# Channel 128's copy and rest on GpSimd instead of VectorE, and the weight decode's last two pieces in chunk 11 instead of chunks 9 and 10

## The chip, the cores and the metric

The kernel runs on one core of one Trainium2 chip. The metric is device time in microseconds (us) of one execution. TensorE is called PE below, VectorE DVE, ScalarE ACT, GpSimd POOL; SP is the engine from which all DMAs here are issued.

## What is computed

The input has two batches of 3136 positions by 256 channels. Three blocks follow one another (cut to what matters):

```python
def reference(**kw):
    # 1: Fourier mixing along the sequence
    X = np.fft.rfft(x, axis=1)
    Yr = Xr @ w_r - Xi @ w_i + b_r;  Yi = Xr @ w_i + Xi @ w_r + b_i
    Y = soft_threshold(Yr, 0.01) + 1j * soft_threshold(Yi, 0.01)
    x = np.fft.irfft(Y, n=3136, axis=1)
    # 2: normalise, two matrix products with a ReLU between, add
    xn = (x - mean) / np.sqrt(var + 1e-6) * g_ln
    x = x + np.maximum(xn @ w_ch1, 0.0) @ w_ch2
    # 3: x plus the real part of a 2D FFT of x, then the same again with other weights
    u = x + np.real(np.fft.fft(np.fft.fft(x, axis=1), axis=2))
    un = (u - mean) / np.sqrt(var + 1e-6)
    return u + np.maximum(un @ w_ch1, 0.0) @ w_ch2
```

## The kernel before

The sequence length is 49 x 64, and each Fourier transform is two matrix products with tables. The program is recorded in one order, and a list scheduler then sets the order on each engine, so moving a step also shifts its neighbours a little.

**The two MLPs.** `mlp1` (block 2) has 13 chunks, numbered 0 to 12, of four tiles of 128 rows each, but for chunk 6 (three tiles) and chunk 7 (two). `mlp2` (block 3) has 13 more. `run_mlp` (L869) goes over them. In each chunk `l1(f)` (L619) makes one of eight slices f of the hidden layer: six matmuls into a PSUM buffer psa, of which there are three. Then ACT writes the rounded ReLU h (L631), and DVE writes the rest that the rounding left (L632), which gives psa back to PE. `l2(i)` (L639) sums the eight slices into psb, and DVE adds the result to the input (L649). The next chunk is normalised by `prep` (L570: a chain of small DVE operations L576 to L585 with one ACT step between) and transposed by `trans` (L599).

**The decode.** The weights of `mlp2` come as 64-bit numbers in eight pieces. `decode64` (L500) turns a piece into two float parts with eight DVE operations of 128x512 (L506 to L514), into the tile r2b. `MLP2_AT` (L26) says in which chunk of `mlp1`, and after which slice f of `l1`, each piece is decoded. The two pieces that the change moves fill the part of r2b that holds `w_ch2`, which is first read by `l2` of `mlp2` chunk 0.

**Stage 4.** `Stage98` (L334) makes the first transform of block 3, for batch 0 from the end of chunk 7 on, in which SP issues its first loads, and for batch 1 during `mlp2` from its chunk 0 on. Its 16 steps each load 98x512 values (L348), fold channels c and 256 - c with three POOL operations (`split`, L360 to L362), round on ACT (L364), take the rest on POOL (L365, seen in the trace as L210), multiply on PE into a buffer psc, of which there are three (`mm3r`, L220 to L222), copy out on ACT (L404) and store. Channel 128 has no partner. `middle` (L369) loads it alone for all steps (98x32 values, tile m), and `middle2` (L376), run with step 0, copies and splits it, multiplies it (L381), and copies the product to the tile `mid`; POOL puts two columns of `mid` into every step's output (L405).

An engine works through its own queue in order. What stands behind a waiting instruction on that engine waits too.

Of the kernel before, what the change touches and what calls it, by code (L numbers as in the profile page):

```python
# [22 lines left out]
STAGE3_AT = (0,) * 16 + (3, 3, 3, 3, 3, 1)  # L23
CONST_AT = (0, 0, 1, 2, 2, 3, 4, 5, 6, 8)
MLP1_AT = (5, 8, 10, 12, 13, 14, 15, 18)
MLP2_AT = ((4, 6), (5, 2), (5, 6), (6, 2), (6, 6), (7, 3), (9, 3), (10, 6))  # L26
STAGE3_END = 3
STAGE3_MLP = ((0, 0), (0, 1), (0, 2), (0, 3), (1, 0), (1, 1), (1, 2), (1, 3),
              (2, 0), (2, 1), (2, 2), (2, 3), (3, 0))
# [25 lines left out]
NQ = 98  # L55
# [107 lines left out]
def fourier_moe_kernel(ctx, tc, x, w_r, w_i, b_r, b_i, g_ln, w11, w12, w21, w22,  # L163
                       t_ca, t_cam, t_cim, t_cb, t_ci, t_cb0, t_ci0, t_cd, t_ident, out):
    nc = tc.nc
# [9 lines left out]
    def psum(tag):  # L175
        return pp.tile([128, 512], F32, tag="ps" + tag, name="ps" + tag, bufs=ps_bufs[tag])
# [24 lines left out]
    def a_copy(o, i, scale=1.0):  # L201
        nc.scalar.activation(out=o, in_=i, func=AF.Copy, scale=scale)

    def v_copy(o, i):
        nc.vector.tensor_copy(o, i)
# [3 lines left out]
    def sub(eng, o, a, b):  # L209
        ins = eng.tensor_tensor(out=o, in0=a, in1=b, op=ALU.subtract)  # L210
        mark["pool" if eng is nc.gpsimd else "dve"] = getattr(ins, "ins", ins)

    def mm3(ps, lh, ll, rh, rl, first, last):
        nc.tensor.matmul(out=ps, lhsT=lh, rhs=rh, start=first, stop=False)  # L214
        nc.tensor.matmul(out=ps, lhsT=lh, rhs=rl, start=False, stop=False)  # L215
        nc.tensor.matmul(out=ps, lhsT=ll, rhs=rh, start=False, stop=last)  # L216
# [117 lines left out]
    class Stage98:  # L334
# [40 lines left out]

        def middle2(self):  # L376
            t, hl = self.mid_in
            v_copy(hl[:, 0], t)
            sub(nc.vector, hl[:, 1], t, hl[:, 0])
            ps = psum(self.tag)  # L380
            mm3(ps[0:NQ, 0:32], cs_h, cs_l, hl[:, 0], hl[:, 1], True, True)  # L381
            self.mid = wk.tile([NQ, 32], F32, tag="mid", name="mid", bufs=1)
            v_copy(self.mid, ps[0:NQ, 0:32])

        def start(self):
            self.middle()
# [531 lines left out]
    def after(k, i, f):  # L918

        def g():  # L920
            with tc.issue_after(mlp1[k].rest[i]):
                f()
        return g
# [8 lines left out]
    def hook(k, part, i, f):  # L932
        hooks.setdefault((k, part, i), []).append(f)

    mlp2_w = load_mlp(w21, w22, r2b, "stg", True)
    hook(4, "l1", 2, mlp2_w[0])
    for (k, i), f in zip(MLP2_AT, mlp2_w[1:]):
        hook(k, "l1", i, after(k, i, f))
# [42 lines left out]
```

## Time and profile before

| | us |
|---|---|
| three runs: median (lowest, highest) | 839.77 (838.01, 841.67) |
| the profiled execution's own time | 835.99 |
| its span, first to last instruction | 834.2 |
| busy in it: PE, DVE, ACT, POOL | 813.7, 499.3, 312.3, 141.1 |
| mean granted clock of PE | 0.998 |

PE is busy for 98% of the span. A change elsewhere can therefore give back only time in which PE stood still, and each such gap has to be looked up by itself. In the rows below a timeline line gives the start, the duration, the engine, the line of the program, the output and inputs, and in brackets how long the engine stood idle before it and what ended that.

### The profile page before, as it was taken

The page shows a single profiled execution, that of the slowest core. Times are in us where ns is not written, and L with a number is a line of the kernel's source. Part 1 is how long each engine was busy: PE and PEld are TensorE (multiplying, and loading weights), DVE is VectorE, ACT ScalarE, POOL GpSimd, SP SyncE. Part 2 cuts the span into 40 slices and gives each one's busy share as a digit, 9 for nine tenths or more (in the row PEclk, how much of TensorE's full clock was granted, in tenths as well). Part 3 has the DMA queues.
Part 4 walks back from the last instruction along what each step waited for, and adds up shares of the span by engine and source line. Part 5 has one row for each costly group of instructions (what it writes and reads, how often), then busy time and mean ns, then how long its engine had stood idle before and what let it go on. Part 6 is the DMA issues. An engine that isn't in the chain of part 4 may idle for free.

```text
span 834.2 us, 13615 instructions
## 1 busy us (share of the span) xinstructions
PE 813.7 (98%) x5240; PEld 716.1 (86%) x5240; DVE 499.3 (60%) x1152; ACT 312.3 (37%) x627; POOL 141.1 (17%) x198
## 2 busy tenths in 40 slices
PE   9999999999999999989999998999999999999997
PEld 3888977868888999959799998899899999999996
DVE  6579995475565578754755345625545566545652
ACT  1322356354343222364553225455532233322221
POOL 0212221320000000097410004345400000000000
PEclk9999999999999999999999999999999999999999
DMA  8642200711014321453133113343232122210001
GB/s 230 215 139 72 76 1 1 244 67 51 23 29 158 127 77 67 116 171 121 56 105 101 64 49 77 109 139 103 86 96 86 46 62 59 70 51 25 18 19 30
DMA packets 48180, 71.66 MB, mean 86 GB/s; under 512 B 11746, under 2 KB 32490, under 8 KB 47920
## 3 DMA queue, kind: packets, MB, share of 16 engines
q1 hardware_dynamic: 48116, 70.80, 27.6%
q8 instruction: 41, 0.67, 0.3%
q14 instruction: 23, 0.19, 0.1%
HBM read 45.09 MB, written 25.69 MB: 85 GB/s over the span
## 4 chain that ended last, share of the span: by engine, by line
PE 81%; DVE 8%; DMA 5%; SPq 2%; ACT 1%; POOL 1%; issue 1%; POOLq 0%; DVEq 0%; ACTq 0%
PE psb L215 11%; PE psb L216 11%; PE psb L214 11%; PE psa L220 10%; PE psa L221 9%; PE psa L222 9%; PE psb L461 4%; PE psc L320 3%; PE psc L708 2%; PE psc L607 2%; PE psc L301 2%; PE psc L481 1%; PE psa L429 1%; DMA h<-in_x_dram 1%; PE psa L733 1%; DVE h L632 1%
## 5 line engine op out<-in xcount | busy, mean ns | idle before, releaser
L631 ACT ACTIVATE h<-psa 128x512 fp32r<-128x512 f32 (+2 forms) x208 | 117.8, 573 | 260.5 <-PE psa L222 240.3
L632 DVE SCALAR_TENSOR_TENSOR h<-psa,h 128x512 fp32r<-128x512 f32 (+2 forms) x208 | 135.0, 654 | 101.0 <-ACT h L631 99.9
L214 PE MATMUL psb<-r2b,h 128*128 128x256 f32 x392 | 111.1, 286 | 0.0
L214 PE MATMUL psb<-r3a,h 128*128 128x256 f32 x392 | 110.1, 284 | 0.0
L215 PE MATMUL psb<-r2b,h 128*128 128x256 f32 x392 | 109.8, 283 | 0.0
L215 PE MATMUL psb<-r3a,h 128*128 128x256 f32 x392 | 109.7, 283 | 0.0
L216 PE MATMUL psb<-r3a,h 128*128 128x256 f32 x392 | 108.2, 283 | 0.0
L216 PE MATMUL psb<-r2b,h 128*128 128x256 f32 x392 | 107.5, 283 | 0.0
L649 DVE TENSOR_TENSOR o<-psb,yb 128x256 f32<-128x256 f32 x74 | 31.0, 424 | 101.8 <-PE psb L216 99.9
L461 PE MATMUL psb<-wm,h 128*128 128x256 f32 (+1 forms) x600 | 88.8, 298 | 1.1 <-DVE w L467 1.1
L220 PE MATMUL psa<-q,r3a 128*128 128x512 f32 (+2 forms) x208 | 83.8, 403 | 4.9 <-DVE h L632 4.8
L220 PE MATMUL psa<-q,r2b 128*128 128x512 f32 (+2 forms) x208 | 82.4, 396 | 3.4 <-DVE h L632 3.4
L461 PEld LDWEIGHTS psb<-wm,h 128*128 128x128 f32 (+1 forms) x600 | 76.1, 189 | 8.9 <-issue 8.3
L221 PE MATMUL psa<-q,r3a 128*128 128x512 f32 (+2 forms) x208 | 78.7, 379 | 0.0
L222 PE MATMUL psa<-q,r3a 128*128 128x512 f32 (+2 forms) x208 | 78.7, 381 | 0.0
L221 PE MATMUL psa<-q,r2b 128*128 128x512 f32 (+2 forms) x208 | 78.2, 378 | 0.0
L222 PE MATMUL psa<-q,r2b 128*128 128x512 f32 (+2 forms) x208 | 78.0, 379 | 0.0
L215 PEld LDWEIGHTS psb<-r3a,h 128*128 128x128 f32 x392 | 74.9, 192 | 1.0 <-issue 0.2
L214 PEld LDWEIGHTS psb<-r3a,h 128*128 128x128 f32 x392 | 74.8, 191 | 1.0 <-issue 0.3
L214 PEld LDWEIGHTS psb<-r2b,h 128*128 128x128 f32 x392 | 74.9, 191 | 0.7
L215 PEld LDWEIGHTS psb<-r2b,h 128*128 128x128 f32 x392 | 75.0, 192 | 0.5
L216 PEld LDWEIGHTS psb<-r3a,h 128*128 128x128 f32 x392 | 74.4, 191 | 0.3
(113 smaller groups left out, 1416.6 us busy)
## 6 DMA issues: line engine op xcount, KB each, us to landing
s<-in_moe_w_ch_dram SPq DMA_DIRECT2D x16, 512.0 KB
r<-dX SPq DMA_DIRECT2D x32, 196.0 KB
dA<-o SPq DMA_DIRECT2D x32, 196.0 KB
dY<-yg SPq DMA_DIRECT2D x12, 512.0 KB
r<-dA SPq DMA_DIRECT2D x48, 128.0 KB
dX<-o SPq DMA_DIRECT2D x11, 512.0 KB
yb<-dX SPq DMA_DIRECT2D x50, 64.0 KB
out_dram<-o SPq DMA_DIRECT2D x50, 64.0 KB
```

What stands on the lines that cost most here:

```text
L214: nc.tensor.matmul(out=ps, lhsT=lh, rhs=rh, start=first, stop=False)
L215: nc.tensor.matmul(out=ps, lhsT=lh, rhs=rl, start=False, stop=False)
L216: nc.tensor.matmul(out=ps, lhsT=ll, rhs=rh, start=False, stop=last)
L220: nc.tensor.matmul(out=ps, lhsT=lh, rhs=rh, start=first, stop=False)
L221: nc.tensor.matmul(out=ps, lhsT=ll, rhs=rh, start=False, stop=False)
L222: ins = nc.tensor.matmul(out=ps, lhsT=lh, rhs=rl, start=False, stop=last)
L301: nc.tensor.matmul(out=ps, lhsT=cam, rhs=self.raw[g // 2][:, e * 512:(e + 1) * 512], start=True, stop=True)
L320: nc.tensor.matmul(out=ps[0:NQ, :], lhsT=cim, rhs=t, start=True, stop=True)
L461: nc.tensor.matmul(out=ps[0:m, u * D:(u + 1) * D], lhsT=xv[:, o:o + m], rhs=wm_hl[wv][:, e, c, :], start=k == 0, stop=k == 11)
L631: nc.scalar.activation(out=h[:, 0:n], in_=ps[:, 0:n], func=AF.Relu)
L632: ins = nc.vector.scalar_tensor_tensor(out=l[:, 0:n], in0=ps[:, 0:n], scalar=0.0, in1=h[:, 0:n], op0=ALU.max, op1=ALU.subtract)
L649: nc.vector.tensor_tensor(out=self.o[:, i, :], in0=ps[:, 0:D], in1=self.y[:, i, :], op=ALU.add)
```

## The change

`middle2`'s copy and rest go to POOL, its last copy to ACT. Pieces 6 and 7 of the decode go from chunk 9 (slice 3) and chunk 10 (slice 6) to chunk 11 (slices 2 and 6).

```diff
-MLP2_AT = ((4, 6), (5, 2), (5, 6), (6, 2), (6, 6), (7, 3), (9, 3), (10, 6))
+MLP2_AT = ((4, 6), (5, 2), (5, 6), (6, 2), (6, 6), (7, 3), (11, 2), (11, 6))
...
         def middle2(self):
             t, hl = self.mid_in
-            v_copy(hl[:, 0], t)
-            sub(nc.vector, hl[:, 1], t, hl[:, 0])
+            nc.gpsimd.tensor_copy(hl[:, 0], t)
+            sub(nc.gpsimd, hl[:, 1], t, hl[:, 0])
             ps = psum(self.tag)
             mm3(ps[0:NQ, 0:32], cs_h, cs_l, hl[:, 0], hl[:, 1], True, True)
             self.mid = wk.tile([NQ, 32], F32, tag="mid", name="mid", bufs=1)
-            v_copy(self.mid, ps[0:NQ, 0:32])
+            a_copy(self.mid, ps[0:NQ, 0:32])
```

The first place is DVE's queue in `mlp2` chunk 0, where stage 4 of batch 1 starts. (h is a slice's rest, mhl channel 128's two parts, w a work tile of the other transform of block 3.)

```order
 L210 TENSOR_TENSOR q<-psc,q 128x512 x2
 L649 TENSOR_TENSOR o<-psb,yb 128x256 x2
-L632 SCALAR_TENSOR_TENSOR h<-psa,h 128x512 x2
-L205 CAST mhl<-m_5173 98x32
-L632 SCALAR_TENSOR_TENSOR h<-psa,h 128x512
-L210 TENSOR_TENSOR mhl<-m_5173,mhl 98x32
+L632 SCALAR_TENSOR_TENSOR h<-psa,h 128x512 x3
 L205 COPY w<-psa 128x2
 L632 SCALAR_TENSOR_TENSOR h<-psa,h 128x512
```

The operation that needs channel 128's load no longer stands between the second and the third L632. On POOL the two operations now stand right ahead of the batch's first L360.

The second place is ACT's queue at the start of chunk 8, where stage 4 of batch 0 starts; before:

```order
L202 ACTIVATE s_1657<-w 98x512 x4
L631 ACTIVATE h<-psa 128x512 x3
L581 ACTIVATE sm<-mv,e_81 128x4
L592 ACTIVATE q<-yb,ng 128x256 x4
L202 ACTIVATE o_1658<-psc 98x512
L593 ACTIVATE q<-q,sm 128x256 x3
L631 ACTIVATE h<-psa 128x512
```

And with the change:

```order
L202 ACTIVATE s_1657<-w 98x512 x4
L631 ACTIVATE h<-psa 128x512
L202 ACTIVATE mid<-psc 98x32
L631 ACTIVATE h<-psa 128x512 x2
L581 ACTIVATE sm<-mv,e_81 128x4
L592 ACTIVATE q<-yb,ng 128x256 x2
L202 ACTIVATE o_1658<-psc 98x512
L592 ACTIVATE q<-yb,ng 128x256 x2
L593 ACTIVATE q<-q,sm 128x256 x2
L631 ACTIVATE h<-psa 128x512
```

The copy to `mid` is new, and two instead of three L593 stand ahead of the fourth L631. On PE the first L222 of stage 4 (step 0) now stands ahead of step 2's L220 and L221, and not behind them.

The third place is DVE's queue in chunk 11, from its second L632 on; before:

```order
L632 SCALAR_TENSOR_TENSOR h<-psa,h 128x512 x2
L649 TENSOR_TENSOR o<-psb,yb 128x256
L632 SCALAR_TENSOR_TENSOR h<-psa,h 128x512 x4
L613 SCALAR_TENSOR_TENSOR q<-psc,g_sb,q 128x512 x2
L632 SCALAR_TENSOR_TENSOR h<-psa,h 128x512
```

With the change (the first of the two pieces; the second follows in the same way around the L613):

```order
L632 SCALAR_TENSOR_TENSOR h<-psa,h 128x512 x2
L506 TENSOR_SCALAR t_4489<-s_3366 128x512
L509 TENSOR_SCALAR t_4490<-s_3366 128x512
L508 SCALAR_TENSOR_TENSOR t_4489<-s_3366,t_4489 128x512
L632 SCALAR_TENSOR_TENSOR h<-psa,h 128x512
L510 SCALAR_TENSOR_TENSOR r2b<-t_4490,t_4489 128x512
L511 TENSOR_SCALAR t_4490<-s_3366 128x512
L513 TENSOR_SCALAR t_4489<-r2b 128x512
L512 SCALAR_TENSOR_TENSOR t_4490<-s_3366,t_4490 128x512
L632 SCALAR_TENSOR_TENSOR h<-psa,h 128x512
L514 SCALAR_TENSOR_TENSOR r2b<-t_4490,t_4489 128x512
L632 SCALAR_TENSOR_TENSOR h<-psa,h 128x512 x2
```

In chunks 9 and 10 the same rows are gone and the L632 stand together. SP's load of piece 7 stays where it was, ahead of the same loads of stage 4.

## Rows read from the trace of the kernel before

**Rows 1.** The page's part 1: busy time, share and instructions of each engine.

```profile
PE 813.7 (98%) x5240; PEld 716.1 (86%) x5240; DVE 499.3 (60%) x1152; ACT 312.3 (37%) x627; POOL 141.1 (17%) x198
```

**Rows 2.** Who waited for whom, PE: us in total, times, longest.

```profile
PE psa L220 <- DVE h L632: 8.2, 10, 2.6
```

**Rows 3.** Timeline of PE: matmuls ahead of which PE stood still.

```profile
361.56 0.47 PE L222 MATMUL psc<-s,ca_hl 98*98 98x512 f32 x1 [0.76 <-POOL s L210]
...
371.06 0.51 PE L220 MATMUL psa<-q,r3a 128*128 128x512 f32 x1 [2.56 <-DVE h L632]
...
404.39 0.50 PE L220 MATMUL psa<-q,r3a 128*128 128x512 f32 x1 [1.57 <-DVE h L632]
...
503.97 0.50 PE L220 MATMUL psa<-q,r2b 128*128 128x512 f32 x1 [2.35 <-DVE h L632]
...
536.24 0.50 PE L220 MATMUL psa<-q,r2b 128*128 128x512 f32 x1 [0.29 <-DVE h L632]
```

**Rows 4.** Timeline of mlp2 chunk 0, DVE and ACT around channel 128's load.

```profile
498.26 0.69 DVE L632 SCALAR_TENSOR_TENSOR h<-psa,h 128x512 fp32r<-128x512 f32 x1 [0.67 <-ACT h L631]
...
498.99 0.60 ACT L631 ACTIVATE h<-psa 128x512 fp32r<-128x512 f32 x1 [0.76 <-PE psa L222]
...
503.14 0.18 DVE L205 CAST mhl<-m 98x32 fp32r<-98x32 f32 x1 [4.19 <-DMA m<-dX]
503.23 0.68 DVE L632 SCALAR_TENSOR_TENSOR h<-psa,h 128x512 fp32r<-128x512 f32 x1
```

**Rows 5.** Timeline of DVE, chunk 9: the decode of piece 6.

```profile
401.95 1.79 DVE L510 SCALAR_TENSOR_TENSOR r2b<-t,t 128x512 fp32r<-128x512 int32 x1
403.66 0.68 DVE L632 SCALAR_TENSOR_TENSOR h<-psa,h 128x512 fp32r<-128x512 f32 x1
```

**Rows 6.** Timeline of DVE, chunk 10: piece 7's first and last operation.

```profile
432.18 0.42 DVE L506 TENSOR_SCALAR t<-s 128x512 int32<-128x512 int32 x1
...
437.47 0.69 DVE L514 SCALAR_TENSOR_TENSOR r2b<-t,t 128x512 fp32r<-128x512 f32 x1
```

**Rows 7.** Busy time by stretch: chunks 5 and 6, chunk 9, chunk 10, chunks 11 and 12.

```profile
core 0: us, PE busy (x) PEld busy (x) DVE busy (x) ACT busy (x) POOL busy (x), PEclk, DMA share, GB/s
...
300.00:344.00 44.00, 44.00 (x322) 42.69 (x321) 36.23 (x91) 12.23 (x28) 0.00 (x0) 1.00 0.23 79
...
398.00:412.00 14.00, 12.33 (x79) 10.64 (x78) 11.24 (x16) 7.63 (x16) 7.34 (x11) 1.00 0.19 59
...
430.00:440.00 10.00, 10.00 (x68) 9.09 (x67) 7.74 (x15) 2.67 (x5) 0.29 (x1) 1.00 0.36 111
440.00:495.00 55.00, 55.00 (x381) 51.15 (x380) 27.38 (x74) 14.27 (x29) 0.00 (x0) 1.00 0.19 61
```

**Rows 8.** Timeline of DVE, start of stage 4, batch 0: channel 128, the decode's end.

```profile
351.83 0.18 DVE L205 CAST mhl<-m 98x32 fp32r<-98x32 f32 x1 [2.54 <-DMA m<-dX]
...
355.28 1.26 DVE L514 SCALAR_TENSOR_TENSOR r2b<-t,t 128x512 fp32r<-128x512 f32 x1
```

**Rows 9.** Timeline of POOL there: the first splits, and the first rests.

```profile
353.08 0.85 POOL L360 TENSOR_TENSOR w<-r 98x254 f32<-98x254 f32 x1 [165.16 <-DMA r<-dX]
...
354.63 0.66 POOL L362 COPY w<-r 98x4 f32<-98x4 f32 x1
...
355.94 1.19 POOL L361 TENSOR_TENSOR w<-r 98x254 f32<-98x254 f32 x1
357.07 0.19 POOL L362 COPY w<-r 98x4 f32<-98x4 f32 x1
...
357.91 0.73 POOL L361 TENSOR_TENSOR w<-r 98x254 f32<-98x254 f32 x1
...
360.24 5.02 POOL L210 TENSOR_TENSOR s<-w,s 98x512 fp32r<-98x512 f32 x4
```

**Rows 10.** Timeline of DVE and ACT, chunk 8: the normalisation ahead of the long wait.

```profile
366.73 1.45 DVE L584 SCALAR_TENSOR_TENSOR sm<-sm 128x4 f32<-128x4 f32 x1
...
368.49 1.31 ACT L593 ACTIVATE q<-q,sm 128x256 f32<-128x256 f32 x3 [0.98 <-DVE sm L585]
```

## The prediction

> **What bounds the kernel now.** I read the busy times first: PE works for 813.7 us of the span of 834.2 [rows 1], so a change beside PE can win back gaps of PE and nothing else. The view of who waited for whom says how much there is: the longest entry, L220 waiting for DVE's L632, is 8.2 us over ten times, 2.6 at the longest [rows 2]. PE's timeline places the gaps [rows 3]: 0.76 and 2.56 where stage 4 of batch 0 starts (chunk 8), 1.57 in chunk 9, 2.35 in `mlp2` chunk 0 where stage 4 of batch 1 starts, and 0.29 in the next chunk of `mlp2`, which comes three times in the same way. Then I looked at what DVE, POOL and ACT did just ahead of each. The gaps were read in an execution of 835.99 us (span 834.2 and 1.8 around it). That is 3.8 below the median of the runs, 839.77, and 2.0 below the lowest. I take the same difference off the median.
>
> **Channel 128 in batch 1.** DVE finishes the L632 of the second slice at about 498.95. ACT has the third slice's ReLU ready at 499.6 (498.99 + 0.60). But the next in DVE's queue is channel 128's copy, which waits 4.19 us for its load until 503.14, and the third L632 only starts at 503.23 [rows 4]. PE needs that L632: psa has three buffers, the transform's matmuls took the second one, and L220 at 503.97 takes the third. Without the copy the third L632 is done at about 500.3, over a microsecond before PE comes to that L220 (503.97 - 2.35 = 501.62). So the whole gap goes. What is late next is the other transform's chain on DVE two slices on, which in the next three chunks, where channel 128 is not loaded, leaves 0.29 [rows 3]. I take that as what remains: 2.35 - 0.29 = **2.06 won**. The bounds are 2.35 and, if another wait fills the place, 0.
>
> **The decode's piece in chunk 9.** DVE's L510 there took 1.79 us and the L632 behind it started at 403.66; PE's L220 at 404.39 waited 1.57 for it [rows 3, 5]. POOL was busy for 7.34 of those 14 us [rows 7], and the other piece, in chunk 10 with POOL at 0.29 of 10 us, left PE busy all 10 [rows 7]. With the piece gone the four L632 stand together and wait for ACT alone: **1.57 won**, bounded by 0 if ACT, which rounds for stage 4 there too, is as late. The piece in chunk 10 costs PE nothing now, so taking it away wins nothing.
>
> **Both pieces in chunk 11.** One piece took DVE from 432.18 to 438.16, 5.98 us, in which three other operations of about 0.68 ran: 3.9 for its eight operations [rows 6]. Two are 7.9 more in a stretch of 55 us in which DVE is busy for 27.38 and POOL for nothing [rows 7]. The cover is the three psa buffers: a slice lasts 1.36 (0.60 + 0.76 between ACT's starts [rows 4]), so PE wants a buffer back two slices, 2.7 us, after it has filled it; ReLU (0.60) and L632 (0.69) take 1.3 of that, and 1.4 is left. The longest unbroken run of decode in the new order is four operations, half a piece, 2.0 us. By that the gap would be 0 to 0.6 per piece. The nearest row speaks for 0: in 300 to 344, where four pieces are decoded, two to a chunk after the same slices 2 and 6, DVE is busy for 36.23 of 44 us and PE for all 44 [rows 7]. **Cost taken: 0**, bounds 0 and 1.2. If the cover failed, the third L632 behind would be the one that PE waits for. The last quarter of r2b is read only in `mlp2` chunk 0, more than 30 us later. The load of piece 7 keeps its place in SP's queue, so no transfer moves, and the loads behind it wait no longer than before.
>
> **Channel 128 in batch 0.** Here DVE waits 2.54 us for the load, until 351.83, but PE has `l2` to do and does not feel it directly. Behind the wait stand the last operations of piece 5, which thereby run beside POOL's first folds; the last, L514, takes 1.26 at 355.28 [rows 8], and POOL's operations are stretched: 0.85, 0.66 and 1.19 where the same ones undisturbed take 0.73, 0.19 and 0.73 [rows 9]. That is 0.12 + 0.47 + 0.46 = 1.05 us. The first rest on POOL starts behind these folds at 360.24, and PE's L222 at 361.56 waited 0.76 for it [rows 3, 9]. With the decode 2.5 us earlier it is over about when POOL starts, so I take the **0.76 as won**. In the gap of 2.56 at 371.06 PE waits for an L632 that waits for a ReLU behind three L593 of 1.31 us together [rows 10]. The new order has two ahead of it: 1.31 / 3 = **0.44 won**. The bounds of this part are 3.32 (both gaps close) and 1.3 lost, one more POOL rest (5.02 / 4 = 1.26 [rows 9]) in the way of DVE's chain.
>
> That last bound rests on a row: DVE's L584, on 128x4 numbers, took 1.45 us while POOL worked [rows 10]. The Trainium skill, "SBUF — State Buffer", section "SBUF: two separate sides", says that GpSimd and a VectorE operation with two inputs in SBUF exclude each other for a whole instruction, and the row agrees. By that rule alone the gap of 2.56 would stay whole unless POOL's rests fall elsewhere, and the sum would lose its 0.44.
>
> **What POOL, ACT and PE get.** The trace has no POOL operation on 98x32. A copy of 98x4 takes 0.19 and a fold of 98x254 takes 0.85 at most [rows 9]; 32 numbers are nearer to 4, so I take 0.25 each. Two end 0.5 after 351.83, while POOL's first fold starts at 353.08 [rows 8, 9]: no cost; at the upper end 0.45 late, which would come off the 0.76. If the load came after the folds' data, the folds would wait behind it; before, it came 1.25 ahead. The copy of `mid` on ACT lies between the 0.18 of DVE's copy [rows 8] and the 0.60 of a 128x512 ReLU [rows 4]. It holds a psc buffer that stage 4's step 2 takes next, but on PE that stands behind the L222 that waits for POOL's 1.26 anyway: cost 0, at most 0.3.
>
> **Sum:** 2.06 + 1.57 + 0.76 + 0.44 = 4.8 us. The profiled execution would be 831.2, and the median 839.77 - 4.8 = **835.0 us**, 0.57% less. About 0.5% (4.2 us) is what a measurement of this kernel can tell from no change.
>
> **The rivals.**
> - *The gaps are filled again.* The order of all three engines shifts in chunks 8 to 10, and DVE's small operations and ACT's roundings meet POOL's work by chance. For it: the 2.56 comes from just that, and in chunk 9 POOL is busy half the time with or without the decode. If chunk 8 loses one POOL rest (1.26) instead of winning 1.2, and chunk 9 wins half (0.8), the sum is 2.06 + 0.8 - 1.26 = 1.6: 838.2 us. Against it: the 2.06 hangs on no such meeting.
> - *The long gap of chunk 8 closes as well.* If DVE's chain there no longer meets a POOL rest, 2.56 goes and not 0.44: 4.8 + 2.1 = 6.9, 832.9 us. For it: its largest step took 1.45 for an operation that does almost nothing. Against it: POOL has as many rests as before.
> - *DVE becomes the bound in chunk 11.* The place is the run of slices 3 to 7, where the decode stands between the L632. If the psa buffers were no cover, both pieces would show on PE: 7.9 - 4.8 = 3.1 slower, 842.9 us. It decides from the point at which more than 4.8 of the 7.9 are exposed. Against it: the 44 us without a gap.
> - *The change does nothing*, if the scheduler gave back the old order. The order shows that it didn't; under 1 in 100.
>
> **The chances.** 0.52 for the forecast, whose own range is 3.2 to 6.0 won, and some three quarters of it lie beyond 4.2; 0.30 for the refilled gaps; 0.12 for the long gap; 0.06 for chunk 11, half of it beyond 4.2 with chunk 8's gains gone too. So faster by over 0.5%: 0.38 + 0.12 = 0.50; within: 0.14 + 0.30 + 0.03 = 0.47; slower: 0.03. The range reaches from a little beyond the long gap's 832.9 to almost no change: 832.2 to 839.6, which leaves out chunk 11 and the tails.
>
> **What would show it.** In the changed profile: no wait of DVE for m; the L632 of `mlp2` chunk 0's third slice starting with its ReLU's end, and a gap of PE there of 0.3 or none; no gap in chunk 9; PE busy without a break where chunk 11 decodes, at 3.9 us of DVE a piece; POOL's two new operations at 0.2 to 0.3 and ahead of the first fold; the gap at the first L222 gone. The prediction is wrong if one of the first three gaps is back behind another waiter, if the gap at 371 grows, or if L220 waits for an L632 behind a decode operation in chunk 11.

## The result, and the profile after

The changed kernel takes **832.9 us** (median of 4 runs, 831.65 to 833.91) where the kernel before takes 839.71 in runs beside it (4 runs, 838.01 to 841.67): a ratio of 0.9917 with an interval of 0.9892 to 0.9943, so 6.8 us less. Two later comparisons, on two chips, gave 0.9962 (0.9948 to 0.9977) and 0.9926 (0.9907 to 0.9945), that is 3.2 and 5.5 us less. It is faster by more than 0.5% in two of the three and by 0.4% in the third. The forecast was 4.8 us, and 835.0. The first comparison's 832.9 is also the number of the rival in which the long gap of chunk 8 closes; that gap did not close, so the agreement is chance.

The profiled execution took 833.91 (span 832.1), only 2.1 below that of before. It is the slowest of its four runs, and the one profiled before was faster than all its other runs, so this pair of profiles shows less than the medians do. The page's part 1:

```profile
PE 814.0 (98%) x5240; PEld 716.6 (86%) x5240; DVE 498.8 (60%) x1146; ACT 312.8 (38%) x629; POOL 140.4 (17%) x202
```

Nothing was saved in work [rows 1]. What PE waited for, us in total, times, longest:

```profile
PE psa L220 <- DVE h L632: 6.2, 7, 2.5
```

That is 2.0 us and three waits less [rows 2]. PE's timeline, the matmuls after 355 with idle time of 0.2 us or more ahead (one more, of 0.28 at 594.25, repeats that at 533.51):

```profile
361.58 0.47 PE L222 MATMUL psc<-s,ca_hl 98*98 98x512 f32 x1 [0.22 <-POOL s L210]
367.31 0.50 PE L220 MATMUL psa<-q,r3a 128*128 128x512 f32 x1 [1.36 <-DVE h L632]
372.16 0.50 PE L220 MATMUL psa<-q,r3a 128*128 128x512 f32 x1 [2.48 <-DVE h L632]
375.45 0.50 PE L220 MATMUL psa<-q,r3a 128*128 128x512 f32 x1 [0.74 <-DVE h L632]
...
533.51 0.50 PE L220 MATMUL psa<-q,r2b 128*128 128x512 f32 x1 [0.28 <-DVE h L632]
564.17 0.50 PE L220 MATMUL psa<-q,r2b 128*128 128x512 f32 x1 [0.88 <-DVE h L632]
```

Against [rows 3]: the gap of 1.57 in chunk 9 is gone, and the one of 2.35 in `mlp2` chunk 0. Of the two in chunk 8 the first shrank from 0.76 to 0.22 and the long one stayed (2.56, now 2.48), but one of 1.36 at 367.31 is new, and 0.74 stands behind the long one, where the kernel before has 0.31 (at 373.94). In `mlp2` chunk 2, 0.88 stands where the kernel before has 0.29.

Around channel 128's load in `mlp2` chunk 0, DVE:

```profile
498.10 0.69 DVE L632 SCALAR_TENSOR_TENSOR h<-psa,h 128x512 fp32r<-128x512 f32 x1 [0.67 <-ACT h L631]
499.46 0.69 DVE L632 SCALAR_TENSOR_TENSOR h<-psa,h 128x512 fp32r<-128x512 f32 x1 [0.67 <-ACT h L631]
```

and POOL, at the start of stage 4 of batch 0 and of batch 1:

```profile
352.89 0.57 POOL L378 CAST mhl<-m 98x32 fp32r<-98x32 f32 x1 [163.81 <-DMA m<-dX]
353.55 0.68 POOL L210 TENSOR_TENSOR mhl<-m,mhl 98x32 fp32r<-98x32 f32 x1
354.19 0.73 POOL L360 TENSOR_TENSOR w<-r 98x254 f32<-98x254 f32 x1
...
503.18 0.39 POOL L378 CAST mhl<-m 98x32 fp32r<-98x32 f32 x1 [63.90 <-DMA m<-dX]
503.65 0.31 POOL L210 TENSOR_TENSOR mhl<-m,mhl 98x32 fp32r<-98x32 f32 x1
504.68 0.73 POOL L360 TENSOR_TENSOR w<-r 98x254 f32<-98x254 f32 x1 [0.72 <-PE psa L733]
```

The third L632 waits for its ReLU and for nothing else, where 4.19 us for the load stood [rows 4]. It is POOL that now waits for the load, and nobody waits for POOL there: in batch 1 POOL still stood idle for 0.72 ahead of its first fold, for PE.

The stretches of [rows 7] that the change touches (us, then busy time of PE, PEld, DVE, ACT, POOL, the granted clock, DMA share and GB/s):

```profile
398.00:412.00 14.00, 13.89 (x88) 12.10 (x87) 7.10 (x14) 8.90 (x19) 7.41 (x14) 1.00 0.21 67
430.00:440.00 10.00, 10.00 (x70) 9.25 (x69) 3.55 (x6) 3.19 (x6) 0.19 (x1) 1.00 0.13 40
440.00:495.00 55.00, 55.00 (x380) 51.02 (x379) 34.70 (x90) 14.07 (x29) 0.00 (x0) 1.00 0.23 76
```

With both pieces in chunk 11, DVE does 34.70 us there and not 27.38, and PE is still busy for all 55.

### The profile page after: what moved, and what is told of

Same layout as the page of the kernel before. It is cut to its first block, busy times and chain, and to the rows that moved or that the text cites. A ratio compares the mean times of both kernels' runs of the same rounds, so it can differ in the third digit from the quotient of the medians.

```text
span 832.1 us, 13607 instructions
## 1 busy us (share of the span) xinstructions
PE 814.0 (98%) x5240; PEld 716.6 (86%) x5240; DVE 498.8 (60%) x1146; ACT 312.8 (38%) x629; POOL 140.4 (17%) x202
## 4 chain that ended last, share of the span: by engine, by line
PE 81%; DVE 9%; DMA 4%; SPq 2%; ACT 1%; POOL 1%; issue 1%; ACTq 0%; DVEq 0%
PE psb L215 11%; PE psb L216 11%; PE psb L214 11%; PE psa L220 10%; PE psa L221 10%; PE psa L222 10%; PE psb L461 3%; PE psc L320 3%; PE psc L708 3%; PE psc L607 2%; DMA h<-in_x_dram 2%; PE psc L481 1%; PE psc L301 1%; PE psa L429 1%; PE psa L733 1%
## 5 line engine op out<-in xcount | busy, mean ns | idle before, releaser
L631 ACT ACTIVATE h<-psa 128x512 fp32r<-128x512 f32 (+2 forms) x208 | 118.0, 574 | 251.1 <-PE psa L222 233.2
L632 DVE SCALAR_TENSOR_TENSOR h<-psa,h 128x512 fp32r<-128x512 f32 (+2 forms) x208 | 134.9, 654 | 101.7 <-ACT h L631 100.3
L216 PE MATMUL psb<-r3a,h 128*128 128x256 f32 x392 | 108.2, 283 | 0.0
L216 PE MATMUL psb<-r2b,h 128*128 128x256 f32 x392 | 107.5, 283 | 0.0
L220 PE MATMUL psa<-q,r3a 128*128 128x512 f32 (+2 forms) x208 | 83.8, 403 | 4.9 <-DVE h L632 4.8
L220 PE MATMUL psa<-q,r2b 128*128 128x512 f32 (+2 forms) x208 | 82.4, 396 | 1.6 <-DVE h L632 1.4
L221 PE MATMUL psa<-q,r3a 128*128 128x512 f32 (+2 forms) x208 | 78.7, 378 | 0.0
L222 PE MATMUL psa<-q,r3a 128*128 128x512 f32 (+2 forms) x208 | 78.7, 381 | 0.0
L221 PE MATMUL psa<-q,r2b 128*128 128x512 f32 (+2 forms) x208 | 78.2, 378 | 0.0
L222 PE MATMUL psa<-q,r2b 128*128 128x512 f32 (+2 forms) x208 | 78.0, 379 | 0.0
L216 PEld LDWEIGHTS psb<-r3a,h 128*128 128x128 f32 x392 | 74.4, 191 | 0.2
```

What stands on the lines that cost most here:

```text
L222: ins = nc.tensor.matmul(out=ps, lhsT=lh, rhs=rl, start=False, stop=last)
L631: nc.scalar.activation(out=h[:, 0:n], in_=ps[:, 0:n], func=AF.Relu)
L632: ins = nc.vector.scalar_tensor_tensor(out=l[:, 0:n], in0=ps[:, 0:n], scalar=0.0, in1=h[:, 0:n], op0=ALU.max, op1=ALU.subtract)
```

## The experiments

### Both kernels again

The kernel before and the changed one, unaltered, among other kernels on one chip, to see how far a time and a profile repeat.

> The kernel before, unchanged, for a second look at its gaps: ratio 1.000. The profiled execution of before (835.99) is 3.7 below the median of its other runs. Theory: the gaps of chunks 8 and 9, where VectorE's and ACT's work meets POOL's by chance, differ by 2 to 4 us in sum between the two profiles. Rival: those are alike, and the difference lies in the first loads (before 25 us) or nowhere in one place.

> The changed kernel, unchanged, for a second look: 832.9, ratio 0.992. Theory: no gap in chunk 9 and none in mlp2 chunk 0 as in its first profile, while chunk 8's gaps (4.98 us in the first profile, 3.98 before) come out differently by up to 2. Rival: chunk 8's 4.98 repeats within 0.2, so that it belongs to the new order and not to chance.

Before again: 839.5 us (12 runs), a ratio of 1.0015 (1.0001 to 1.0028) to the same kernel's 26 runs beside it, 838.14. So a difference of 1.3 us tells nothing here. The change again: 834.93 (833.15 to 835.23, 7 runs), 0.9962 (0.9948 to 0.9977). The gaps of chunks 8 and 9 differ by 1.2 us between the two profiles of the kernel before, not by the 2 to 4 expected, and the change's chunk 8 has 4.46 where it had 4.98. The profiles held something that the first ones had not. In that of before again, PE's timeline has both long gaps:

```profile
371.35 0.50 PE L220 MATMUL psa<-q,r3a 128*128 128x512 f32 x1 [2.67 <-DVE h L632]
...
505.50 0.50 PE L220 MATMUL psa<-q,r2b 128*128 128x512 f32 x1 [2.59 <-DVE h L632]
```

and the stretches of 1 us around the second one (the granted clock is the third number from the end) show that the clock fell behind it:

```profile
504.00:505.00 1.00, 0.00 (x0) 0.00 (x0) 0.33 (x2) 0.00 (x0) 0.00 (x0) 1.00 0.54 97
505.00:506.00 1.00, 0.50 (x2) 0.46 (x3) 1.00 (x4) 0.29 (x2) 0.00 (x0) 0.97 0.81 299
506.00:507.00 1.00, 1.00 (x3) 0.72 (x3) 0.93 (x5) 0.23 (x2) 0.71 (x2) 0.50 0.02 6
507.00:508.00 1.00, 1.00 (x4) 0.79 (x3) 1.00 (x2) 0.00 (x0) 1.00 (x3) 0.50 0.00 0
508.00:509.00 1.00, 1.00 (x4) 0.80 (x3) 0.47 (x2) 0.60 (x1) 0.92 (x2) 0.50 0.00 0
509.00:510.00 1.00, 1.00 (x5) 0.78 (x5) 1.00 (x3) 0.00 (x0) 0.91 (x3) 0.82 0.63 166
```

From 506 to 509 PE runs at 0.50, its lower level of 1.2 GHz, and is back at 2.4 GHz a little after 509. The loss is 0.03 + 3 x 0.50 + 0.18 = 1.71 us of full clock. The same sum over 372 to 380, behind the first gap, is 1.72. In the first profile of before neither stretch shows it. So the price of such a gap is its length, and in some executions up to 1.7 us more. The two falls are 3.4 us of full clock together. PE's busy time is 816.1 us there and not the 813.7 of [rows 1], so 2.4 us of them reach the time, in an execution that took 839.13 where the first took 835.99.

Every run has a mean granted clock beside its time, so this can be followed beyond the profiles. A fall of this size takes 0.002 off the mean over the span (1.71 of 836), from the 0.998 of the first profile, which has none before its last 4 us. Of 72 runs of the kernel before (12 here, 60 beside the experiments) 33 have 0.994 or less and took 840.2 us on average; 22 have 0.995 to 0.997 and 17 more than that, and both groups took 837.7 (837.67 and 837.65). Of the change's 16 runs none is below 0.995, and they took 833.6. One fall alone does not show in these times; two or more do.

### Each part alone

The channel's part alone (the decode's table as before):

```diff
-MLP2_AT = (..., (7, 3), (11, 2), (11, 6))
+MLP2_AT = (..., (7, 3), (9, 3), (10, 6))
```

> Channel 128's part of the change alone; the decode stays in chunks 9 and 10. Theory (the gaps are as the profile of before shows them): the 2.35 us gap of mlp2 chunk 0 is gone, chunk 8 moves by -1.2 to +1.3, the 1.57 in chunk 9 stays: 836.4 to 838.9, ratio about 0.9975. Rival (the measured gain of 6.8 comes mostly from the decode meeting POOL's work, in unprofiled runs worse than in the profiled one): little is won here, 838.5 or more.

Measured: 834.48 (7 runs), 0.9954 (0.9934 to 0.9974): 2 us below the range expected. The gap of `mlp2` chunk 0 is gone, that of chunk 9 stays, and `mlp2` chunk 2 has its short one:

```profile
405.86 0.50 PE L220 MATMUL psa<-q,r3a 128*128 128x512 f32 x1 [1.55 <-DVE h L632]
...
565.23 0.50 PE L220 MATMUL psa<-q,r2b 128*128 128x512 f32 x1 [0.28 <-DVE h L632]
```

The decode's part alone (the kernel before with the new table):

```diff
-MLP2_AT = (..., (7, 3), (9, 3), (10, 6))
+MLP2_AT = (..., (7, 3), (11, 2), (11, 6))
```

> The decode's part alone; channel 128's copy and rest stay on VectorE. Theory: the 1.57 us gap of chunk 9 is gone, no gap appears in chunk 11, the 2.35 of mlp2 chunk 0 stays: about 838.1, ratio 0.998. Rival: 835 or less, with two thirds or more of the whole gain. With e1: if the two gains add up to about 6.8, the parts are independent; if they add up to 3.6, something needs both.

Measured: 838.1 (12 runs), 1.0001 (0.9986 to 1.0016). The time is the 838.1 expected, but only because the kernel before took 838.14 here; the ratio expected was 0.998. The gap of chunk 9 is gone, that of `mlp2` chunk 0 stands at 2.72, with the clock at 0.85 and 0.72 in the two stretches of 4 us around and behind it (500 to 504, 504 to 508):

```profile
502.67 0.70 PE L220 MATMUL psa<-q,r2b 128*128 128x512 f32 x1 [2.72 <-DVE h L632]
```

So channel 128 alone gives what the whole change gives on that chip (834.48 against 834.93). The decode's part takes its gap away in the profile, and no time goes with it that these runs can tell: against the kernel before it is 0.0 us, against *before again* 1.4 less, and those two are the same kernel.

### Each batch's channel 128 alone

The changed kernel, with one batch's copy, rest and last copy back on DVE. Of the batch 1 kernel the core is (batch 0's has `dX1[0]`):

```diff
+            on_dve = self.src is dX1[1]
-            nc.gpsimd.tensor_copy(hl[:, 0], t)
-            sub(nc.gpsimd, hl[:, 1], t, hl[:, 0])
+            (nc.vector if on_dve else nc.gpsimd).tensor_copy(hl[:, 0], t)
+            sub(nc.vector if on_dve else nc.gpsimd, hl[:, 1], t, hl[:, 0])
...
-            a_copy(self.mid, ps[0:NQ, 0:32])
+            (v_copy if on_dve else a_copy)(self.mid, ps[0:NQ, 0:32])
```

> The changed kernel with channel 128 of batch 1 alone back on VectorE (batch 0 stays on GpSimd, the decode in chunk 11). Theory: TensorE's gap in mlp2 chunk 0 comes back (2.4 to 2.7 us), and behind it the granted clock falls for some us in a part of the executions, as in two of the three profiles that had this gap: 2.4 plus 0 to 2 slower than the changed kernel, ratio to before 0.999 to 1.001, with more scatter than the changed kernel. Rival (a gap costs its length): 2.5 slower, ratio 0.999, no more scatter. Second rival (batch 0's part carries the gain): ratio still 0.996.

Measured: 836.77 (834.69 to 841.03, 12 runs), 0.9982 (0.9961 to 1.0003), where 0.999 to 1.001 was expected: not told from the kernel before. The gap is back, and its clock with it (PE's timeline, then stretches of 4 us; this edit adds a line, so that L632 is L633 here and L589 is L590):

```profile
503.37 0.79 PE L220 MATMUL psa<-q,r2b 128*128 128x512 f32 x1 [2.56 <-DVE h L633]
```

```profile
500.00:504.00 4.00, 1.44 (x8) 1.11 (x7) 1.46 (x6) 1.30 (x4) 0.00 (x0) 0.88 0.56 111
504.00:508.00 4.00, 4.00 (x16) 3.22 (x15) 3.03 (x9) 0.78 (x3) 3.49 (x6) 0.69 0.17 49
```

The scatter is back too: 6.3 us between the 12 runs, where the change itself had about 2 in its 4, 7 and 5.

> The changed kernel with channel 128 of batch 0 alone back on VectorE. Theory: the gain hangs on batch 1; here chunk 8's gaps differ by less than 1 us either way: ratio to before 0.995 to 0.997, as the changed kernel. Rival (VectorE's wait of 2.5 us in chunk 7 costs as much as that in batch 1): ratio 0.998 or more.

Measured: 833.83 (832.26 to 836.18, 7 runs), 0.9938 (0.9913 to 0.9963), as good as the whole change, and 2.9 us below the batch 1 kernel, measured beside it. The first gap of chunk 8 is back, and there is none in `mlp2` chunk 0:

```profile
361.22 0.47 PE L222 MATMUL psc<-s,ca_hl 98*98 98x512 f32 x1 [0.77 <-POOL s L210]
```

So batch 0's part shortens that gap and is worth nothing that the time shows; **batch 1's part carries the gain**.

### What keeps the gaps of chunk 8

Chunk 9's normalisation, done during chunk 8, put on DVE, so that ACT's normalising steps L592 and L593 go there and no ReLU stands behind them:

```diff
-    for ch in mlp1[8:12] + mlp2[1:5]:
+    for ch in mlp1[8:9] + mlp1[10:12] + mlp2[1:5]:
         ch.by_act = True
```

> The changed kernel, but chunk 9's rows are normalised on VectorE (four operations of 128x256) and no longer on ScalarE (eight), so that in chunk 8 no ReLU stands behind them in ScalarE's queue. Theory: chunk 8's gap of 2.5 us is gone or under 1, the granted clock no longer falls at 372 to 380, 2 to 4 us faster than the changed kernel: ratio to before 0.991 to 0.994. Rival (VectorE's chain, held by GpSimd, is late in any case, and now the L632 stand behind it): the gap stays at 2 or more behind VectorE, ratio 0.996 or above.

Measured: 835.87 (12 runs), 0.9959 (0.9941 to 0.9977), where 0.991 to 0.994 was expected, and one gap of 6.40 us at 375.11, as in the rival: the L632 now stand behind DVE's chain. DVE's timeline:

```profile
365.03 1.65 DVE L583 SCALAR_TENSOR_TENSOR sm<-mv,sm 128x4 f32<-128x4 f32 x1
366.72 1.49 DVE L584 SCALAR_TENSOR_TENSOR sm<-sm 128x4 f32<-128x4 f32 x1
368.24 0.18 DVE L585 RECIPROCAL sm<-sm 128x4 f32<-128x4 f32 x1
368.45 6.01 DVE L596 TENSOR_SCALAR q<-yb,mv,sm 128x256 f32<-128x256 f32 x4
374.38 1.87 DVE L632 SCALAR_TENSOR_TENSOR h<-psa,h 128x512 fp32r<-128x512 f32 x3
```

Four L596 take 6.01 us; with POOL idle, four such take 1.38 in the kernel before:

```profile
444.25 1.38 DVE L596 TENSOR_SCALAR q<-yb,mv,sm 128x256 f32<-128x256 f32 x4
```

So ACT's queue alone does not hold the gap: these operations of DVE are stretched beside POOL's work, L583 and L584 too, with or without ACT. That POOL is the cause the next kernel shows.

In it POOL's first four rests of batch 0 went to DVE:

```diff
-            sub(nc.gpsimd, l, f, h)
+            sub(nc.vector if g < 4 and self.src is dX1[0] else nc.gpsimd, l, f, h)
```

> The changed kernel, but the first four rests of stage 4 of batch 0 are taken on VectorE and not on GpSimd, so that GpSimd's four operations of 1.26 us no longer lie beside the normalisation in chunk 8. Theory (VectorE's small operations wait for GpSimd's long ones): L589, L583 and L584, 2.29, 0.79 and 1.48 us in the changed kernel, fall below 0.8 each, the 1.34 us gap goes and the 2.5 us gap shrinks by 1 or more: ratio to before 0.992 to 0.995. Rival: GpSimd's other operations of 0.73 hold them as long, and VectorE has four operations more: ratio 0.996 or above.

Measured: 831.28 (830.2 to 832.96, 6 runs), 0.9906 (0.9879 to 0.9933), a little better than expected. DVE's small operations there:

```profile
364.66 0.28 DVE L589 TENSOR_SCALAR ng<-mv 128x4 f32<-128x4 f32 x1
...
365.05 0.71 DVE L583 SCALAR_TENSOR_TENSOR sm<-mv,sm 128x4 f32<-128x4 f32 x1
365.79 0.66 DVE L584 SCALAR_TENSOR_TENSOR sm<-sm 128x4 f32<-128x4 f32 x1
```

L589 takes 0.28 where the changed kernel has 2.29, and L584 0.66 where it has 1.48. The long gap fell to 0.88, the one of 1.36 to 0.66. In their place PE waits 1.95 for ACT's copy of `mid`:

```profile
361.35 0.47 PE L220 MATMUL psc<-s,ca_hl 98*98 98x512 f32 x1 [1.95 <-ACT mid L202]
...
371.54 0.50 PE L220 MATMUL psa<-q,r3a 128*128 128x512 f32 x1 [0.88 <-DVE h L632]
```

That copy stands in ACT's queue behind the roundings of the first four steps, these wait for POOL's folds, and POOL's copies in the folds are slow beside DVE's rests (a rest takes 1.23 on DVE):

```profile
354.85 1.26 POOL L362 COPY w<-r 98x4 f32<-98x4 f32 x1
```

It ends at 356.11, as DVE's L514 behind the rest does (356.06). The next three such copies take 0.65 to 0.67, and 27 of the 32 take 0.18 to 0.25. So POOL is held by DVE as DVE is by POOL. The Trainium skill, "SBUF — State Buffer", section "SBUF: two separate sides", says that GpSimd and a DVE operation with two inputs in SBUF hold the port they share for a whole instruction each; L583, L584 and the rests, which are such operations, agree with it.

### The version with the rests on DVE, and three beside it

That kernel again, the change again beside it, and two variants of it: with the decode's pieces back in chunks 9 and 10, and with batch 0's channel 128 back on DVE. Their edits are those above, put together.

> The changed kernel with the first four rests of stage 4's batch 0 on DVE, again (the kernel of e8), beside the change itself (e10) on the same chip. Theory (a long gap of PE costs its own length, and in some executions a stretch of the lower granted clock behind it as well): no gap over 2.0 us in chunk 8, no stretch from 360 to 384 under a granted clock of 0.99, median 2 to 4 us below e10's, scatter of the runs under 3 us. Rival (only the length of gaps counts): median below e10's by the difference of the gaps in chunk 8 alone, 0.5 to 1.2 us.

Measured: 832.61 (831.18 to 833.85, 6 runs), 0.9918 (0.9898 to 0.9937).

> The change again, unaltered, so that the other three stand beside it on one chip. Both theories: ratio to the kernel before between 0.991 and 0.997; gaps of 4.3 to 5.0 us in chunk 8, none in chunk 9 and in mlp2 chunk 0. Theory of the clock: if the profile shows a dip, it lies from 372 to 380, behind the gap of 2.5, and nowhere between 480 and 520.

Measured: 833.35 (832.04 to 833.65, 5 runs), 0.9926 (0.9907 to 0.9945), gaps of chunk 8 as in the first profile (0.27, 1.37, 2.48, 0.72), no fall of the clock.

The version with the rests on DVE is 0.7 us below the change, where the theory had 2 to 4 and its rival 0.5 to 1.2, and the intervals lie over one another. It does win its gaps, but the theory's second half fell: its longest gap, 1.95 us, was followed by a fall of the clock in this profile (stretches of 4 us):

```profile
360.00:364.00 4.00, 2.06 (x9) 1.30 (x8) 3.17 (x5) 1.83 (x4) 4.00 (x7) 1.00 0.75 229
364.00:368.00 4.00, 3.67 (x11) 2.39 (x10) 3.96 (x14) 3.05 (x7) 4.00 (x8) 0.71 0.81 278
368.00:372.00 4.00, 4.00 (x17) 3.15 (x16) 1.44 (x4) 4.00 (x10) 4.00 (x7) 0.87 0.65 191
```

In the earlier profile of the same kernel it was not. A shorter gap alone does not keep the clock up.

> As e9, but with the decode's last two pieces back in chunks 9 and 10. Theory (the decode's part is worth its gap, 1.57 us): the gap of about 1.57 in chunk 9 is back behind DVE's L632, nothing new in chunk 11, and the median is 1.0 to 2.0 us above e9's. Rival (the decode's part is worth nothing in the time, as its run alone suggested): the gap is back in the profile and the median stays within 0.6 us of e9's. A third way: with the rests out of POOL's queue the gap does not come back at all, and the two are the same.

Measured: 831.91 (831.07 to 832.82, 4 runs), 0.9912 (0.9891 to 0.9933): 0.7 below the kernel with the decode in chunk 11, so if anything the wrong way. Chunk 9 shows a gap of 0.59 and not 1.57, ahead of L216:

```profile
405.30 0.39 PE L216 MATMUL psb<-r3a,h 128*128 128x256 f32 x1 [0.59 <-DVE h L632]
```

The theory that the decode's part is worth its gap gets no support here either; but as only 0.59 of the gap came back, this run can't test the whole 1.57.

> As e9, but batch 0's channel 128 is copied, split and copied out on DVE as in the kernel before; batch 1's stays on GpSimd and ACT. In e8 PE waited 1.95 us at 361 for ACT's copy of mid. Theory (that wait is ACT's place in the queue, and DVE gives mid back earlier): this gap falls to 0.8 or less, chunk 8's gaps come to 2 to 3 us where e8 had 4.0, and the median is 1 to 2 us below e9's. Rival (the next waiter, POOL's first s or DVE's L632 behind channel 128's load, fills the place): chunk 8's gaps stay at 3.5 to 4.5 us and the median within 0.6 us of e9's; should one gap there be over 2.3 us again, a dip of the clock behind it, and more scatter.

Measured: 831.77 (831.52 to 832.01, 4 runs), 0.991 (0.989 to 0.993). The gap did not shrink but grew:

```profile
364.07 0.44 PE L220 MATMUL psc<-s,ca_hl 98*98 98x512 f32 x1 [2.81 <-DVE mid L205]
```

`mid` is now behind DVE's fourth rest. The theory fell on the gap; the rival had the gaps of chunk 8 about right (4.6 us), but the clock did not fall behind 2.81 us here, and the scatter did not grow. The time is the lowest of the four, but by 0.1 from the next one, so none of the three variants is told from another, and against the change itself they gain 0.7 to 1.6 us, which is about what this measurement can tell.

## Why the forecast held, point by point

**Batch 1's channel 128 (2.06 forecast): right, and worth more than its length.** The gap went from 2.35 to none, and the 0.29 that I had left for the next late chain did not come in that chunk. Taking this part away cost the gain again (836.77). What the term leaves out is the clock. Four profiles have this gap (before, before again, the decode alone, batch 1 on DVE), and in three of them the clock falls behind it; ten do not have it, and in none of them does the clock move between 495 and 515. So the term is 2.35 us of waiting or more (2.35 to 2.72), and in three profiles of four up to 1.7 on top. With that a premise of mine falls: a change beside PE can win back not only time in which PE stands still, but also time in which it is busy at the lower clock.

**Chunk 9's decode (1.57 forecast): the gap went, the time was not seen.** PE's gap is gone in every kernel with the new table. But the decode alone measured 1.0001, the whole change is no faster than channel 128 alone (834.93 against 834.48), and taking the decode back out of the version with the rests on DVE cost nothing. The traces show where part of the 1.57 goes. Behind 340 PE's gaps of 0.15 us or more come to 6.8 us with channel 128 alone and to 6.4, 5.9 and 6.5 in the change's three profiles, so the decode's part is worth 0.4 to 0.9 net there. The 0.88 of `mlp2` chunk 2 stands in these three profiles and in no other: DVE's L742 takes 0.78 beside POOL's folds there, and 0.42 with channel 128 alone. The 0.74 in chunk 8 stands in two of the three. The step that failed in this term is that the gap's length comes off the time. Whether the rest is lost too or lies below what these runs resolve stays open.

**Chunk 11 (cost 0): right.** PE 55.00 of 55 us, DVE 7.3 us more (7.9 forecast). That no transfer would move was wrong, at no cost: the first of the other transform's loads behind 430 us (L692) goes out at 444.57 and not at 435.85.

**Batch 0's first gap (0.76): mis-sized, 0.54.** POOL's rests do start earlier, at 360.23 and so 10.97 after the first short gap of PE at 349.26; before it was 360.24, 12.15 after the one at 348.09. That is 1.18 earlier, 1.05 was forecast. But PE came earlier as well, since step 0's L222 now stands ahead of step 2's L220 and L221.

**The long gap of chunk 8 (0.44): the term that failed.** I took one L593 less ahead of the ReLU for 0.44, as if DVE's chain ahead of the L593 kept its times. It did not: L585, which releases them, starts at 369.72 and not at 368.21. The gap gave 0.08, and a gap of 1.36 appeared ahead of it. The cause is one operation on 128x4 numbers. DVE's timeline, the changed kernel:

```profile
364.37 2.29 DVE L589 TENSOR_SCALAR ng<-mv 128x4 f32<-128x4 f32 x1
366.58 0.68 DVE L632 SCALAR_TENSOR_TENSOR h<-psa,h 128x512 fp32r<-128x512 f32 x1
```

and the kernel before:

```profile
364.38 0.91 DVE L589 TENSOR_SCALAR ng<-mv 128x4 f32<-128x4 f32 x1
365.20 0.68 DVE L632 SCALAR_TENSOR_TENSOR h<-psa,h 128x512 fp32r<-128x512 f32 x1
```

POOL in the changed kernel:

```profile
360.23 5.04 POOL L210 TENSOR_TENSOR s<-w,s 98x512 fp32r<-98x512 f32 x4
365.24 0.73 POOL L360 TENSOR_TENSOR w<-r 98x254 f32<-98x254 f32 x1
365.92 0.72 POOL L361 TENSOR_TENSOR w<-r 98x254 f32<-98x254 f32 x1
366.58 0.19 POOL L362 COPY w<-r 98x4 f32<-98x4 f32 x1
```

L589 starts 4.14 us after POOL's first rest in both, as (to 0.01) in every profile that keeps the rests on POOL and has an L589 there. It ends either with the fourth rest (before, the decode alone, batch 0 on DVE: 0.90 to 0.91), or two operations of POOL later, with L361 (2.28 to 2.32: the change in all three profiles, the channel alone, batch 1 on DVE, and *before again*). So the new gap is the price of losing a turn against POOL, 1.38 us, and the kernel before loses it in one profile of two. Set beside *before again*, whose gaps of chunk 8 come to 5.18 us, the change's three profiles have 4.98, 4.46 and 5.02: batch 0's part is worth 0.2 to 0.7 us there and not 1.2; set beside the first profile of before, with its 3.98, it costs 0.5 to 1.0. With batch 0's channel 128 on POOL all five such profiles lose the turn, without it one of four. Why, with starts that agree to 0.01 us, stays open.

**POOL's two operations (0.25 each): mis-sized at no cost.** They take 0.31 to 0.68, inside the bounds of 0.19 to 0.85. In batch 0 they end at 354.23; if the two loads land 1.25 apart as in the kernel before, the first fold's data are there at 352.89 + 1.25 = 354.14 (an estimate), so the fold loses next to nothing. ACT's copy of `mid` takes 0.19 and 0.18.

**The sum.** PE's gaps behind 340 (those of 0.15 us or more) fell from 8.9 to 6.4 us in the first pair of profiles: 2.35 + 1.57 - 1.0 (chunk 8) - 0.6 (the 0.88) + 0.2 (short ones), 2.5 where 4.8 was forecast. Between the second pair, *before again* and the change again, they fell from 10.4 to 5.9, 4.4. The medians fell by 6.8, 3.2 and 5.5. The runs' mean clocks split the gain: all 72 runs of the kernel before average 838.8 and the change's 16 runs 833.6, 5.2 less, but the 39 that have no lower clock than the change's runs average 837.7, 4.0 above the change. So about 4.0 us come with the clock alike, and 1.2 with runs of the kernel before at a lower clock; whether the clock itself costs all of that, or longer gaps in the same runs too, the times do not tell. That the number came out right is therefore partly luck: one term failed, one did not show in the time, and the clock, which the sum did not have, about fills their place. Why the three comparisons differ by as much as they do is not explained.

**The rivals.** The refilled gaps came true by half: chunk 8 lost a POOL turn (1.0 net, 1.26 priced), but chunk 9 won its whole gap. The long gap of chunk 8 did not close, though that rival's mechanism was right: with the rests off POOL it fell to 0.88. DVE did not become the bound in chunk 11.

## What to carry to other kernels

An operation that waits for a transfer belongs in the queue of an engine with nothing urgent behind it: here batch 1's two small operations, about twice as slow on POOL (0.39 and 0.31 against 0.18 each), win 2 us and more, because the DVE queue behind them fed PE. A long gap of PE may cost more than its length, so price its removal by several profiles of the same kernel, and look at the granted clock behind the gap; the mean clock of every run shows about how much it fell. And where DVE's small operations meet a stretch of POOL work, expect their durations to jump by whole POOL instructions from one execution to the next, and do not count a gap that hangs on that as won or lost from one profile.

## What the runs showed of the hardware that I had not expected

- **The clock falls behind some gaps and not behind others of the same length.** Behind PE's first 340 us the 14 profiles have 18 gaps of 1.8 us or more. At ten of them (1.91, 1.95, 2.49 twice, 2.54, 2.56, 2.59, 2.67, 2.72, 6.40) the granted clock falls to 0.50, 1.2 GHz, for some 3.4 us (6.8 at the gap of 6.40). The fall begins between 1.9 us before the gap's end (again at 6.40) and 1.9 us after it (at 1.95). At eight (1.84, 1.95, 2.35, 2.47, 2.48 twice, 2.56, 2.81) it stays at 1.00. At shorter gaps, up to 1.57, it never falls there. Each fall takes 1.7 us of full clock, that of the gap of 6.40 3.4. What of it lies inside the gap costs nothing more, and part can hide a later wait, so it is the upper end of what the time loses (2.4 of 3.4 in *before again*). The Trainium skill, "TensorE: Matmul & The Clock Gate", Part 1, says that the clock's level follows how busy PE has been lately; that it falls behind idle time agrees, what decides between two equal gaps no run here shows.
- **A DVE operation on 128x4 numbers can lose more than one turn to POOL:** with the same start beside the same POOL work L589 took 0.90 to 0.91 us in three profiles and 2.28 to 2.32 in six; with the rests off POOL it took 0.18 to 0.28.
- **On POOL the copy of 98x32 takes 0.21 to 0.42 and its rest 0.31 to 0.34** in `mlp2`; at the end of chunk 7 they take 0.38 to 0.62 and 0.25 to 0.68. On DVE each takes 0.18 or 0.19, but for one rest of 0.30.
